# A spectral filter beside 32-head attention on one core: row transform by even and odd rows, Q's second half packed last, and new numbers in the planner

## The chip, the core and the metric

The kernel runs on one core of a Trainium2 chip. A core has five engines that run side by side, each with its own instruction queue: PE multiplies matrices and writes into PSUM (eight banks of 128 x 512 f32), ACT computes functions such as the exponential, DVE does elementwise work, POOL does slower elementwise work, and SP issues DMA transfers. The working memory is SBUF. The metric is the time of one launch on the device in microseconds; the kernel before takes 767.13 us, the median of three runs (766.32 to 768.4).

## The reference

Two independent computations stand beside each other in the output. A is a filter in the frequency domain; B is self-attention with 32 heads of width 20.

```python
def _A_ref(x, w_r, w_i):                       # x: (1, 2048, 640)
    X = rfft2(x.astype(float32), axes=(-2, -1))
    X = X * (w_r + 1j * w_i)                   # weights: (2048, 321)
    return irfft2(X, s=(S, D), axes=(-2, -1)).astype(bfloat16)

def _B_ref(x, wqkv, wo):                       # x: (1, 2048, 640)
    q, k, v = split_heads(x @ wqkv)            # 3 x 32 heads x (2048, 20)
    p = softmax(q @ k.T * 20 ** -0.5, axis=-1) # 2048 x 2048 per head
    return merge_heads(p @ v) @ wo

out = concatenate([a, b], axis=-1)
```

## The kernel before

The order of all instructions is written out ahead of time by a planner in the kernel's Python code. It plays the kernel through with a cost for each instruction, and at each moment puts on each engine what is ready and ranks first. What comes out is a fixed order for each engine, with semaphore waits where data cross engines. The costs decide only the order; the times in this document are the chip's.

**Attention.** There are 32 units, each of one quarter of Q's rows (512) and a group of four heads (list `UNITS`): first quarters 0 and 1 with groups 0 to 3, then quarter 0 and quarter 1 with groups 4 to 7, then quarters 2 and 3. A unit has 16 x 4 score tiles of 128 x 512. PE computes a tile with 32 of its 128 rows (`score_mm`, L821). Most tiles go in pairs to ACT for the exponential (`try_exp`, L1418). The rest go in batches of four to DVE, which builds the exponential from integer operations: four L955, one L998, one L997, one L1005. The product with V (L1076) uses 32 columns of PE per head. At the end of a unit DVE evicts the sum (L1107), the row sums go through DRAM and back as reciprocals (SP), POOL multiplies (L1128), and the output projection follows (L1222, L1233).

**Projection.** Heads 0 to 7 of K, and of the first two quarters of Q, are projected straight into place (L614). The rest is "packed": `packed` computes 128 columns of K or Q for 512 rows of x (five matmuls, L643), DVE evicts them into a staging buffer `stg` (L655), and when a column block is complete `spread_heads` sends each head's 20 rows to its place with a DMA. 34 packed jobs come in the order K1, Q1, K2, Q2, K3, Q3, K4, Q4 with four jobs each, and the last two row quarters of Q0; two staging buffers alternate. `kq_keys` says which pieces a score tile waits for. V is projected by L690. The transposes of x (L592) come ahead of all.

**Filter.** x is folded by POOL (L1630 to L1637), and when all packing is done and spread, the filter runs as background work: row transform S1 (L1736, evicted by L1742), column transform and weights S2 (L1793, L1824), inverse rows S3 (L1896; L1910, L1918, L1923), inverse columns S4 (L1948; L1956, L1967). S1 multiplies 1024 folded rows by four tables of cosine and sine for even and odd frequencies: 4 tables x 5 column blocks x 8 matmuls. Its jobs may start from due times that spread over `FT0` to `FT1` in proportion to the matmul cost. S3 already splits its table into two halves and gets the second half of its output as a difference, in mirrored order.

**Background work and the clock.** `step_pe` first feeds ACT, then uses the room until ACT needs the next pair for products with V, background jobs by priority, and tiles for DVE. Background jobs and DVE's tiles share four PSUM banks. If nothing else can be done and PE's work in the last `WIN` = 3413 ns is under `WARM` times `WIN`, `keep_warm` issues a matmul on constants (L1507), whose result nobody reads.

**SP's queue.** `step_aux` takes the first transfer whose data are there. `put_dma` counts 450 ns for each issue.

Of the kernel before, what the change touches and what calls it, by code (L numbers as in the profile page):

```python
# [255 lines left out]
S = 2048  # L256
D = 640
H = 32
# [39 lines left out]
class KB:  # L298
# [8 lines left out]
    WARM = 0.60  # L307
# [95 lines left out]
    def alloc_filter(self):  # L403
# [17 lines left out]
        self.VX = a.bf(zD + 8 * FBC, 4 * FBC).rearrange("p (s r l) -> p s r l", s=2, r=2)  # L421
        self.X24 = a.bf(zD + 16 * FBC, 8)
# [10 lines left out]
    def put(self, eng, fn, occ, r=(), w=(), pw=(), name="", lat=None, mode="B"):  # L433
        t = self.P.add(eng, fn, r=r, w=w, pw=pw, name=name)
        st = self.free[eng]
        if eng == "pe" and mode != self.mode:
            st += self.SW
            self.mode = mode
            self.switches += 1
        st = max(self.now, st)  # L440
        if eng == "pe":
            while (self.win + 1) * self.WIN + self.PHASE <= st:
                self.cold = self.wacc.get(self.win, 0.0) < self.COLD * self.WIN
                self.ncold += self.cold
                self.win += 1
            self.wacc[self.win] = self.wacc.get(self.win, 0.0) + occ
            self.plog.append((st, occ))
            if self.cold:
                occ *= 2.0
        if eng == "dve" and name in ("p2", "p3", "p4") and self.free["pool"] > st:  # L450
            occ += min(self.free["pool"] - st, 1.8 * occ) * 0.44
        end = st + occ
        self.free[eng] = end
        self.busy[eng] += occ
        if lat is None:
            lat = {"pe": self.L_PE, "act": self.L_ACT, "dve": self.L_DVE, "pool": self.L_POOL}[eng]
        t.vis = end + lat
        self.at(end)
        self.at(t.vis)
        return t  # L460

    def put_dma(self, fn, nbytes, r=(), w=(), pw=(), name="dma", stream=None, out=False):
# [7 lines left out]
        self.free["sp"] = st + 450.0  # L470
        self.dma_free = max(self.dma_free, st + 450.0) + nbytes / rate
        t.vis = self.dma_free + 1900.0
# [105 lines left out]
    def jobs_B(self):  # L578
# [56 lines left out]
        def packed(which, c, kc, sb, free):  # L635
# [15 lines left out]
            def mkev(bank):  # L651
                o = self.stg[sb][:, kc * 512:(kc + 1) * 512]
# [3 lines left out]
            ev = [(mkev, 610.0, [("z", "C", 0)], [("stg", which, c, kc)], [("stgb", sb, kc)], False)]  # L656
            return Job("pk%d" % which, 0.0, pe, ev)
        sb = 0
        hist = []
        order = [(1, 1), (0, 1), (1, 2), (0, 2), (1, 3), (0, 3), (1, 4), (0, 4), (0, 0)]  # L660
        for n_, (which, c) in enumerate(order):
                js = []
                free = hist[-2] if len(hist) >= 2 else []
                hist.append(self.spread_keys(which, c))
                for kc in (range(2, 4) if (which, c) == (0, 0) else range(4)):
                    j = packed(which, c, kc, sb, free)
                    j.prio = 1000.0 + 10 * n_ + kc
                    j.rel = self.PJ0 + self.PJ1 * (n_ + 0.25 * kc)
                    js.append(j)
                    J[("pk", which, c, kc)] = j  # L670

                def post(job, which=which, c=c, sb=sb, js=js):
                    if any(not x.done for x in js):
                        return
                    self.spread_heads(which, c, sb)
                for j in js:
                    j.post = post
                sb = (sb + 1) % 2
# [29 lines left out]
    def spread_keys(self, which, c):  # L708
        nm = ("QT", "KT")[which]
        ks = []  # L710
        for h in range(H):
            lo, hi = max(20 * h, 128 * c), min(20 * h + 20, 128 * c + 128)
            if lo < hi and not (which == 1 and h < 8):
                ks.append((nm + "h", h, c))
        return ks

    def spread_heads(self, which, c, sb):
        dst = (self.QT, self.KT)[which]
        nm = ("QT", "KT")[which]
        for h in range(H):  # L720
            lo, hi = max(20 * h, 128 * c), min(20 * h + 20, 128 * c + 128)
            if lo >= hi:
                continue
            g, j = divmod(h, 4)
            s0 = 0
            if g < 2:
                if which == 1:
                    continue
                s0 = 1024
            d0 = 32 * j + lo - 20 * h  # L730
            o = dst[d0:d0 + hi - lo, g, s0:2048]
            i_ = self.stg[sb][lo - 128 * c: hi - 128 * c, s0:2048]
            self.dma(o, i_, (hi - lo) * (2048 - s0) * 2, r=[(nm + "m", g)] + [("stg", which, c, kc) for kc in range(s0 // 512, 4)] + [("stgb", sb, kc) for kc in range(s0 // 512, 4)] + [("z", "C", 0)],
                     w=[(nm + "h", h, c)], name="spread")

    def kq_keys(self, u, kt):
        qc, g = UNITS[u]
        if g < 2:
            ks = [("KT", g, kt // 4)]
            if qc < 2:  # L740
                ks.append(("QT", g, qc))
            else:
                ks += [("QTh", h, c) for h in range(4 * g, 4 * g + 4) for c in range(20 * h // 128, (20 * h + 19) // 128 + 1)]
            return ks
        ks = []
        for h in range(4 * g, 4 * g + 4):
            c0, c1 = 20 * h // 128, (20 * h + 19) // 128
            for c in range(c0, c1 + 1):
                ks += [("KTh", h, c), ("QTh", h, c)]
        return ks  # L750
# [739 lines left out]
    def keep_warm(self):  # L1490
        t0 = self.now - self.WIN
        u = 0.0
        for st, occ in reversed(self.plog):
            if st + occ < t0:
                break
            u += min(occ, st + occ - t0)
# [50 lines left out]
    def step_aux(self, en):  # L1547
        lst = self.aux[en]
        for i, a in sorted(enumerate(lst), key=lambda x: x[1][6] != "onorm") if en == "pool" else enumerate(lst):
# [92 lines left out]
    def filter_tables(self):  # L1642
# [5 lines left out]
        for par in range(2):  # L1648
            k = 2 * np.arange(512, dtype=np.int64) + par
            ang = th * ((s[:, None] * k[None, :]) % S)  # L1650
            c_, n_ = np.cos(ang), np.sin(ang)
            m_ = -n_
            if par == 0:
                m_[:, 0] = alt
            for m in (c_, m_):
                t1.append(m.reshape(8, 128, 512).transpose(1, 0, 2))
# [42 lines left out]
    def jobs_A(self, after, need):  # L1699
# [16 lines left out]
        def load_x():  # L1716
            for i in range(2):
                self.dma(self.xf[i], self.xs[i].rearrange("(t p) d -> p t d", p=128), 1310720, r=[("xs", i, t) for t in range(8)], w=[("xf", i), zr("A", 0)], name="ld_xA")
# [6 lines left out]
        for idx in range(4):  # L1725
            ri, par = idx % 2, idx // 2
            b = idx % 2
            js = []
            for c in range(5):
                pe = []  # L1730
                for t in range(8):
                    def mk(bank, t=t, c=c, par=par, b=b):
                        o = ps[:, bank, :]
                        l = self.xf[par][:, t, c * 128:(c + 1) * 128]
                        r_ = self.tabs[b][:, t, :]
                        return lambda e: e.matmul(o, l, r_, start=(t == 0), stop=(t == 7))  # L1736
                    pe.append((mk, 216.0, [("xf", par), ("t1", idx), ("t1b", b), zr("A", 1), zr("C", 1)]))

                def mkev(bank, c=c, ri=ri, par=par):
                    o = self.X1[:, c, ri, par * 512:(par + 1) * 512]  # L1740
                    in_ = ps[:, bank, :]
                    return lambda e, en: e.tensor_copy(o, in_)  # L1742
                ev = [(mkev, 608.0, [zr("B", 1)], [("X1", c, ri, par), zr("B", 0)], [], False)]
                js.append(add(Job("S1", 0.0, pe, ev, after=after)))
            S1 += js
            if idx == 1:
                def fix():
                    x1 = self.X1
                    kk = [("X1", c, 1, 0) for c in range(5)]
                    self.pool_op(lambda e: e.tensor_copy(self.X24[:, 0:5], x1[:, :, 1, 0]), 120.0, r=kk + [zr("D", 2), zr("B", 1)], w=[("X24",), zr("D", 1)], name="x24")  # L1750
                    self.pool_op(lambda e: e.memset(x1[:, :, 1, 0], 0.0), 120.0, r=[("X24",), zr("B", 1)], w=kk + [("X1f",)], name="x24z")
                hook("fix", js, fix)
            if idx < 2:
                hook("ldt%d" % (idx + 2), js, (lambda idx: lambda: load_t(self.tabs, self.c_t1, idx + 2, 1, "t1", []))(idx))
# [29 lines left out]
        hook("ldfd", S1[10:15], load_fd)  # L1784
# [14 lines left out]
        for kc in range(9):  # L1799
            i = kc % 2  # L1800
            js = []
            M = 128 if kc < 8 else 1
            for pl in range(4 if kc < 8 else 2):
                sg, ri = divmod(pl, 2)
                if kc < 8:
                    if ri == 0:
                        terms = [(0, 0, t, t) for t in range(3)] + [(1 if sg == 0 else 2, 1, 2 + t, t) for t in range(3)]
                    else:
                        terms = [(0 if sg == 0 else 3, 1, t, t) for t in range(3)] + [(2, 0, 2 + t, t) for t in range(3)]
# [3 lines left out]
                for n, (tab, r_, c, t) in enumerate(terms):  # L1813
# [3 lines left out]
                    ks = [("X1", c, r_, kc // 4), ("X1f",)] if r_ < 2 else [("X24",), zr("D", 2)]  # L1817
# [8 lines left out]
                ev = [(mkev, 65 + 1.042 * 2 * FBC, wkeys(kc, sg) + [zr("D", 2)] + prevY_keys(kc), [(nm, sg), zr("D", 1)], [], False)]  # L1826
# [160 lines left out]
    FT1 = 745000.0  # L1987
# [141 lines left out]
    def build(self):  # L2129
# [7 lines left out]
        for h in range(H):  # L2137
            for c in range(20 * h // 128, (20 * h + 19) // 128 + 1):
                need.append(("QTh", h, c))
                if h >= 8:  # L2140
                    need.append(("KTh", h, c))
# [56 lines left out]
```

## Time and profile before

| | us |
|---|---|
| median of 3 runs | 767.13 |
| the profiled execution, whole | 769.53 |
| its span, first to last instruction | 767.7 |
| PE busy | 734.2 (96%) |
| ACT busy | 729.5 (95%) |
| DVE busy | 669.4 (87%) |
| POOL busy | 132.1 (17%) |

The groups of instructions that the change touches, from part 5 of the profile and the full table of groups:

| line, engine | what | count | busy us |
|---|---|---|---|
| L643 PE | packed projection | 170 weight loads | 44.8 |
| L1736 PE | row transform S1 | 160 weight loads | 41.8 |
| L1742 DVE | S1 evictions | 20 | 13.6 |
| L1507 PE | constant matmuls | 18 | 6.1 |
| L821 PE | scores | 2048 | 309.2 |

Some matmul records are missing from the trace (149 of L643, 140 of L1736), so the weight loads are counted. Durations of matmuls overlap, since each starts before the one ahead of it has drained; their sum says more than the time they take up. The stages of the filter stand one behind the other: S1 from 273 to 441 us, S2 to 528, S3 from 538 to 653, S4 from 660 on.

### The profile page before, as it was taken

The numbers are of one execution on the slowest core, as the hardware profiler recorded it, in microseconds if no ns is written. First come the engines' busy times: TensorE is split into PE (matmuls) and PEld (weight loads), VectorE is DVE, ScalarE is ACT, GpSimd is POOL, SyncE is SP. The second block draws the span as 40 slices with busy tenths as digits, with TensorE's granted clock in tenths as the row PEclk, the third lists the DMA queues.
The fourth block names the chain that finished last, engine by engine and source line by source line (L and its number), as shares of the span: only waits on it lengthen the run. The fifth ranks groups of instructions, "written<-read, shape, count | busy, mean of one in ns | idle before, by whom it ended". The sixth has DMA issues, their size and how long they took to land.

```text
span 767.7 us, 16364 instructions
## 1 busy us (share of the span) xinstructions
PE 734.2 (96%) x6532; PEld 237.0 (31%) x6591; DVE 669.4 (87%) x1234; ACT 729.5 (95%) x797; POOL 132.1 (17%) x142
## 2 busy tenths in 40 slices
PE   8999999999999999999999999999999999999997
PEld 4422233242332222232222333332232322333334
DVE  3598978989788989888989999999998889899895
ACT  5899989999899999999999999999999999999992
POOL 7388840000000000003100121210000000000000
PEclk9999989999999999999999999999999999999999
DMA  9022322110212351212120111212001110211102
GB/s 317 14 68 84 91 74 63 35 47 21 62 33 44 93 216 29 71 45 100 35 72 22 43 51 29 55 35 99 24 20 46 38 31 18 74 56 37 54 19 72
DMA packets 43009, 46.76 MB, mean 61 GB/s; under 512 B 16470, under 2 KB 36312, under 8 KB 42416
## 3 DMA queue, kind: packets, MB, share of 16 engines
q1 hardware_dynamic: 42160, 44.35, 19.1%
q0 software_dynamic: 768, 1.32, 0.7%
q8 instruction: 53, 0.87, 0.5%
q14 instruction: 28, 0.23, 0.1%
HBM read 30.57 MB, written 8.36 MB: 51 GB/s over the span
## 4 chain that ended last, share of the span: by engine, by line
ACT 65%; PE 26%; DVE 6%; DMA 1%; issue 1%; SPq 0%
ACT arena L1418 65%; PE ps L821 8%; PE ps L1076 6%; DVE arena L955 2%; PE ps L1793 2%; PE ps L614 2%; PE ps L690 2%; PE ps L643 2%; PE ps L1222 1%; DVE arena L998 1%; PE ps L1896 1%; DMA arena<-ct 1%; DVE arena L997 1%; PE ps L1948 1%; PE ps L572 1%
## 5 line engine op out<-in xcount | busy, mean ns | idle before, releaser
L1418 ACT ACTIVATE arena<-ps 128x1024 f16<-128x1024 f32 x784 | 722.3, 1126 | 15.8 <-PE ps L821 12.3
L955 DVE TENSOR_SCALAR arena<-ps 128x512 int16<-128x512 f32 x480 | 320.5, 683 | 45.2 <-PE ps L821 43.0
L821 PE MATMUL ps<-arena 32*128 32x512 bf16 x2048 | 309.2, 385 | 13.4 <-ACT arena L1418 8.8
L1076 PE MATMUL ps<-arena 128*32 128x512 f16 x3008 | 236.0, 386 | 1.7 <-DVE arena L998 0.3
L821 PEld LDWEIGHTS ps<-arena 32*128 32x128 bf16 x2048 | 76.2, 91 | 297.4 <-ACT arena L1418 274.9
L1128 POOL TENSOR_TENSOR arena<-arena 128x512 bf16<-128x512 f32 x30 | 39.3, 1309 | 499.3 <-DMA arena<-rd 499.2
L998 DVE TENSOR_SCALAR arena<-arena 128x2048 int16<-128x2048 int16 x120 | 91.0, 758 | 1.4
L997 DVE TENSOR_SCALAR arena<-arena 128x2048 int16<-128x2048 int16 x120 | 86.7, 723 | 3.5 <-PE ps L1076 2.8
L1076 PEld LDWEIGHTS ps<-arena 128*32 128x32 bf16 x3008 | 50.5, 94 | 96.4 <-issue 65.9
L643 PE MATMUL ps<-arena 128*128 128x512 bf16 x149 | 44.8, 383 | 2.2 <-issue 1.7
L1736 PE MATMUL ps<-arena 128*128 128x512 bf16 x140 | 41.8, 383 | 3.4 <-issue 2.4
L1793 PE MATMUL ps<-arena 128*128 128x322 bf16 (+1 forms) x198 | 37.7, 303 | 0.2 <-DVE arena L955 0.2
L1948 PE MATMUL ps<-arena 128*128 128x320 bf16 (+1 forms) x192 | 34.6, 302 | 0.0
L690 PE MATMUL ps<-arena 128*128 128x160 bf16 x320 | 31.3, 240 | 1.6 <-DVE arena L955 1.5
L1896 PE MATMUL ps<-arena 128*128 128x512 bf16 (+3 forms) x121 | 29.8, 332 | 2.1 <-issue 1.3
L1824 DVE TENSOR_TENSOR arena<-ps,arena 128x644 bf16<-128x644 f32 (+1 forms) x34 | 27.9, 822 | 2.1 <-PE ps L1793 1.7
L1005 DVE TENSOR_SCALAR arena<-arena 128x96 bf16<-128x96 bf16 x120 | 29.3, 245 | 0.0
L1222 PE MATMUL ps<-arena 128*128 128x320 bf16 (+1 forms) x152 | 28.2, 302 | 0.6 <-DVE arena L955 0.4
L690 PEld LDWEIGHTS ps<-arena 128*128 128x128 bf16 x320 | 22.3, 100 | 13.2 <-issue 10.4
L696 DVE CAST arena<-ps 128x320 bf16<-128x320 f32 x32 | 15.5, 488 | 11.9 <-PE ps L690 11.8
L655 DVE TENSOR_SCALAR arena<-ps 128x512 bf16<-128x512 f32 x34 | 23.1, 679 | 2.7 <-PE ps L643 2.5
L1107 DVE COPY arena<-ps 128x512 f32<-128x512 f32 (+1 forms) x33 | 21.9, 666 | 1.5 <-PE ps L1076 1.4
(77 smaller groups left out, 354.0 us busy)
## 6 DMA issues: line engine op xcount, KB each, us to landing
arena<-rd SPq DMA_DIRECT2D x120, 64.0 KB
out_dram<-arena SPq DMA_DIRECT2D x32, 160.0 KB
arena<-ct SPq DMA_DIRECT2D x4, 1024.0 KB
arena<-arena SPq DMA_DIRECT2D x42, 80.0 KB
arena<-in_A_x_dram SPq DMA_DIRECT2D x16, 160.0 KB
xs<-arena SPq DMA_DIRECT2D x16, 160.0 KB
arena<-xs SPq DMA_DIRECT2D x2, 1280.0 KB
arena<-arena SPq DMA_DIRECT2D x105, 20.0 KB
```

Source lines behind the costliest of these rows:

```text
L643: return lambda e: e.matmul(o, l, r_, start=(cc == 0), stop=(cc == 4))
L690: return lambda e: e.matmul(o, l, r_, start=st, stop=(c == 4), skip_group_check=True)
L821: return e.matmul(self.ps[:, bank, :], self.KT[32 * j:32 * j + 32, g, kt * 128:(kt + 1) * 128], self.QT[32 * j:32 * j + 32, g, qc * 512:(q ...
L955: return e.tensor_scalar(o, in_, 0.0, 31744.0, ALU.max, ALU.min)
L997: self.dve_push([(lambda e, en: e.tensor_scalar(Ii, Ii, SH2, 0.0, ALU.subtract, ALU.max), occ, ik + pk, ik, [], "p3")], lambda: push(self. ...
L998: ops = [(lambda e, en: e.tensor_scalar(Gi, Ii, SH1, 0.0, ALU.subtract, ALU.max), occ, ik, [("G", b)], [], "p2")]
L1076: inst = e.matmul(self.ps[32 * j:32 * j + 32, bank, :], v_, p_, start=s_, stop=False, tile_position=(0, 32 * j), skip_group_check=True)
L1128: self.pool_op(lambda e: e.tensor_tensor(on, of, bc, ALU.mult), 1600.0, r=pk + [("bcu", u, j) for j in range(4)] + [("bc", j) for j in ran ...
L1418: self.put("act", lambda e: e.activation(o, in_, AF.Exp, bias=ACT_BIAS, scale=ACT_SCALE), 0.8333 * 512 * n + 60.0, r=[("ps", b) for b in b ...
L1736: return lambda e: e.matmul(o, l, r_, start=(t == 0), stop=(t == 7))
L1793: return lambda e: e.matmul(o, lhs, r_, start=st, stop=sp)
L1948: return lambda e: e.matmul(o, l, r_, start=(n == 0), stop=(n == 5))
```

## The change

The change has four parts.

1. **S1** is split by the parity of the row. A frequency k and its mirror 1024 - k have the same sum over even rows and the opposite sum over odd rows (signs aside). So each table now holds 256 cosines and 256 sines for even rows and the same for odd rows: two tables of 1 MB in place of four. For each parity of k and each of five column blocks there are two jobs of four matmuls. The even job is copied to an f32 buffer `sb1`; the odd job's PSUM bank is added to it (first half of the output) and subtracted from it (second half, in mirrored order). For even k three operations on one column go with it. `X24`, which POOL copied before, is written by one of these. In S2 two signs change for the mirrored half.
2. **Packing**: the order becomes K1, the first half of Q1, K2, first half of Q2, and so on to 4, and then the second halves of Q0 to Q4. K has one staging buffer, Q's halves use parts of both. A head of Q is spread by two transfers, one for each half, where it was one.
3. **Planner's DMA costs**: issue times by kind (`ISSUE`), later arrival for some kinds (`LATE`), and an order of kinds in SP's queue (`FIRST`).
4. **Constant matmuls**: a score group counts half (`fillA` 0.5) in the work of the last window, and `WARM` goes from 0.60 to 0.55. `FT1` goes from 745 to 700 us.

```diff
-    WARM = 0.60
+    WARM = 0.55
...
+        self.sb1 = a.f32(zD, 512)
...
-            self.plog.append((st, occ))
+            self.plog.append((st, occ, 0.5 if name == "fillA" else 1.0))
...
+    ISSUE = {"spread": 770.0, "packO": 770.0, "sum": 290.0, "bcast": 465.0}
+    LATE = {"sum2": 1500.0, "spread": 800.0, "ld_tab": 1000.0, "ld_W": 1000.0, "bcast": 500.0}
+    FIRST = {"sum": 0, "sum2": 0, "rec2": 0, "bcast": 0, "spread": 2}
...
-        self.free["sp"] = st + 450.0
-        self.dma_free = max(self.dma_free, st + 450.0) + nbytes / rate
-        t.vis = self.dma_free + 1900.0
+        oc = self.ISSUE.get(name, 530.0)
+        self.free["sp"] = st + oc
+        self.dma_free = max(self.dma_free, st + oc) + nbytes / rate
+        t.vis = self.dma_free + 1900.0 + self.LATE.get(name, 0.0)
...
-        order = [(1, 1), (0, 1), (1, 2), (0, 2), (1, 3), (0, 3), (1, 4), (0, 4), (0, 0)]
-        for n_, (which, c) in enumerate(order):
+        last = {}
+        order = []
+        for c in range(1, 5):
+            order += [(1, c, (0, 1, 2, 3), 0, 0), (0, c, (0, 1), 1, 2 * (c % 2))]
+        order += [(0, c, (2, 3)) + sl for c, sl in enumerate(((1, 2), (0, 0), (0, 2), (1, 0), (1, 2)))]
+        for n_, (which, c, kcs, sb, s0) in enumerate(order):
                 js = []
-                free = hist[-2] if len(hist) >= 2 else []
-                hist.append(self.spread_keys(which, c))
-                for kc in (range(2, 4) if (which, c) == (0, 0) else range(4)):
-                    j = packed(which, c, kc, sb, free)
+                sl = {kc: s0 + i for i, kc in enumerate(kcs)}
+                free = sorted({k for i in sl.values() for k in last.get((sb, i), ())})
+                last.update({(sb, i): self.spread_keys(which, c, kcs) for i in sl.values()})
+                for kc in kcs:
+                    j = packed(which, c, kc, sb, sl[kc], free)
                     j.prio = 1000.0 + 10 * n_ + kc
-                    j.rel = self.PJ0 + self.PJ1 * (n_ + 0.25 * kc)
+                    j.rel = self.PJ0 + self.PJ1 * 0.25 * sum(k[0] == "pk" for k in J)
...
-        for st, occ in reversed(self.plog):
+        for st, occ, wt in reversed(self.plog):
             if st + occ < t0:
                 break
-            u += min(occ, st + occ - t0)
+            u += wt * min(occ, st + occ - t0)
...
+            k = 2 * np.arange(256, dtype=np.int64) + par
+            m = []
+            for e in range(2):
+                se = s[e::2]
+                ang = th * ((se[:, None] * k[None, :]) % S)
+                c_, m_ = np.cos(ang), -np.sin(ang)
+                if par == 0:
+                    mid = th * ((se * 512) % S)
+                    m_[:, 0] = np.rint(np.cos(mid)) if e == 0 else np.rint(np.sin(mid))
+                m.append(np.concatenate([c_, m_], 1))
+            t1.append(np.concatenate(m, 0).reshape(8, 128, 512).transpose(1, 0, 2))
...
+                for e in range(2):
+                    pe = []
+                    for n in range(4):
...
+                            return lambda e: e.matmul(o, l, r_, start=(n == 0), stop=(n == 3))
+                        pe.append((mk, 216.0, [("xf", par, e)] + t1k))
+                    if e == 0:
+                        def mkev(bank):
+                            return lambda e, en: e.tensor_copy(sb1, ps[:, bank, :])
+                        ev = [(mkev, 608.0, prev + [zr("D", 2)], [("sb1", c, par), ("sb1",)], [] if prev else [zr("D", 1)], False)]
+                    else:
...
+                        def e1(bank, X=X, o0=o0):
+                            return lambda e, en: e.tensor_tensor(X[:, :, o0:o0 + 256], ps[:, bank, :].rearrange("p (r k) -> p r k", r=2), sv, ALU.add)
...
+                            return lambda e, en: e.tensor_tensor(X[:, :, 1023:767:-1], sv, i_, ALU.subtract)
...
+                        ev.append((e2, 608.0, kr, [("X1r", c, par)], zw, False))
+                        prev = [("X1r", c, par)]
...
-    FT1 = 745000.0
+    FT1 = 700000.0
```

## Prediction, before the changed kernel was run

> **What bounds the kernel now.** I read the page first. One line of its part 2 and two of part 5:
>
> ```profile
> ACT  5899989999899999999999999999999999999992
> ...
> L1418 ACT ACTIVATE arena<-ps 128x1024 f16<-128x1024 f32 x784 | 722.3, 1126 | 15.8 <-PE ps L821 12.3
> L955 DVE TENSOR_SCALAR arena<-ps 128x512 int16<-128x512 f32 x480 | 320.5, 683 | 45.2 <-PE ps L821 43.0
> ```
>
> ACT computes exponentials almost without a break: 784 of them fill 722.3 us, so one costs 722.3/784 = 0.921 us and covers two score tiles. It is idle 15.8 us before them. The other 480 of the 2048 tiles are done by DVE in batches of four. A batch costs DVE four L955 (4 x 0.67 us), one L997 and one L998 (0.72 + 0.76) and one L1005 (0.24), 4.4 us in all, and spares ACT two exponentials, 1.84 us. PE shows 96% busy, but matmul records overlap; what tells is that ACT waited for it only 12.3 us.
>
> So three things make the span: the number of exponentials, the gaps between them, and the ends before the first and after the last. ACT's own timeline shows the gaps, as pieces with the wait before each in brackets:
>
> ```profile
> 96.45 1.94 ACT L1418 ACTIVATE arena<-ps 128x1024 f16<-128x1024 f32 x2 [0.49 <-PE ps L821]
> 99.95 1.02 ACT L1418 ACTIVATE arena<-ps 128x1024 f16<-128x1024 f32 x1 [1.56 <-PE ps L821]
> ...
> 211.69 62.44 ACT L1418 ACTIVATE arena<-ps 128x1024 f16<-128x1024 f32 x68 [3.92 <-PE ps L821]
> 274.33 232.58 ACT L1418 ACTIVATE arena<-ps 128x1024 f16<-128x1024 f32 x253 [0.21 <-PE ps L821]
> 508.68 68.18 ACT L1418 ACTIVATE arena<-ps 128x1024 f16<-128x1024 f32 x74 [1.77 <-PE ps L1076]
> 577.07 173.92 ACT L1418 ACTIVATE arena<-ps 128x1024 f16<-128x1024 f32 x189 [0.22 <-PE ps L1076]
> ```
>
> Exponentials run from 13.40 to 751.0 us. The gaps that matter are six between 96 and 106 us (0.49 + 1.56 + 0.49 + 0.16 + 0.50 + 0.57 = 3.8 us), one at 208 us (3.9) and one at 507 us (1.8); 3.8 us more lie before 37 us, in the start-up. After 751.0 come 16.7 us. The timeline of the end:
>
> ```profile
> 758.64 4.25 PE L1948 MATMUL ps<-arena 128*128 128x320 bf16 x30
> 758.83 0.43 ACT L1233 CAST arena<-ps 128x320 bf16<-128x320 f32 x1 [1.22 <-PE ps L1227]
> ...
> 762.93 1.01 DVE L1967 TENSOR_TENSOR arena<-arena,ps 128x320 bf16<-128x320 f32 x2
> ```
>
> Attention's last eviction (L1233) ends at 759.26. What ends last is the filter: 30 matmuls of its last stage are left over until attention is through, the last eviction ends at 763.94, and the store behind it closes the span at 767.7.
>
> **Row transform by even and odd rows.** Today 160 matmuls of 512 columns (L1736). In the timeline three such in a row take 0.82 us and two 0.60, so one more costs 0.22. 80 go away: 80 x 0.22 = 17.6 us of PE. None of it is on ACT's path by itself; it lies between 273 and 441 us, where ACT waits for nothing. What it buys is room: the filter's work is fed into PE's gaps, by due times from 200 to 745 us, and it runs late. Before and after are the planner's intended starts, from the job costs in the code (34.6 us, 27.1, 23.0, 26.1 by stage): the last stage is due from 200 + 545 x 84.7/110.8 = 617 us and starts at 660. With 17.3 us in the first stage and an end at 700 it is due from 200 + 500 x 67.4/93.5 = 560. The first stage took 168 us for 160 matmuls; at the same pace 80 take 84. The other stages keep their lengths (90, 123 and 105 us), so the filter ends some 80 us earlier, or at its due time near 700: in both cases before attention does. The leftover after 758.64 then goes. Late next is attention's own store: 759.26 plus the 3.76 us that the last store now takes from its eviction to the end gives 763.0. **Minus 4.7 us.** From below: 0, if the filter stays late; from above nothing more, as the attention tail remains.
>
> The price is on DVE. Twenty copies (L1742, 13.6 us) become ten copies, ten sums and ten mirrored differences, and 15 operations of one column. The third stage of the filter is already built so, and its rows price them: copy L1910 0.680, sum L1918 0.681, difference L1923 0.680, one column L1913 0.150 us. 30 x 0.68 + 15 x 0.15 = 22.6, plus 9.0 us. The 4.5 us of evictions now done after 759 us also move in beside attention. From 273 to 751 us DVE is busy 150.0 + 85.2 + 111.7 + 87.4 = 434.4 of 478 us, 90.9%. To keep all 480 tiles it would have to do 434.4 + 13.5 = 448 us, 93.7%. If the share stays at 90.9%, 13.5/4.4 = 3.1 batches go back to ACT: plus 5.6 us. If it rises to the 94.7% of the fullest stretch (85.24 of 90 us, 442 to 532), there is room for one batch more: minus 1.8. DVE's largest wait is for L821 score matmuls, 43.0 us in 74 waits, and a lighter PE shortens just these; so I take the middle, one batch lost. **Plus 1.8 us.** The two table loads that go away (2 MB) and one POOL copy (0.58 us) cost nothing now: ACT's gap at 274 us is 0.21.
>
> **Q's second half last.** The gap at 208 us is a wait for data. Attention's unit 8 (first quarter of Q, heads 16 to 19) needs the packed projection of columns 256 to 511 of K and Q. In today's order that is job 24 of 34. Weight loads of L643 by windows (five to a job) put its end at 206 us, and its spread transfers and the arrival behind it: ACT resumes at 211.69. Job 18, where the new order has the same data for the first half of Q, was through at 183 us. That is 23 us of margin against a stall of 3.9, so it goes. **Minus 3.9 us.** Nothing else is moved ahead of it: the V jobs keep their places by priority. The second half is first read by unit 16; at 22.6 us a unit (49 tiles x 0.46) that is near 13 + 16 x 22.6 = 375 us, while all packing is over at 254 today. The K staging buffer becomes single: K of the next column block can't be evicted before the last one's seven transfers have landed, about 7 x 0.77 + 3 = 8 us. Two Q jobs and V jobs stand between, and today a job takes (206 - 63)/24 = 6 us, so I cost it at nothing; without that cover it is 8 us for each of three blocks, spread over a margin of 23.
>
> Every transfer is issued by SP. Splitting Q makes 36 + 27 = 63 spread transfers into 27 + 27 + 36 = 90. The queue's rows show twelve of them in 9.17 us, 0.76 each: 27 x 0.76 = 20.6 us more of SP between 62 and 265 us. SP is free there about a third of the time (in a stretch of 22 us a unit costs it some 7.5 us, the 63 spreads add 5 us, loads and stores of the folded input 2). What could be queued behind is the chain of row sums and reciprocals. The new order of SP's queue puts these first and spreads last, so it is cost at nothing. Only POOL's L1128 waits for that chain (499.2 us in 28 waits, nobody behind it in a hurry).
>
> **Issue times and constant matmuls.** The measured issue costs and lateness change only the order that is planned. Where the planner counts a transfer later than it counted it before, it moves other work ahead instead of stalling; no row prices this. It could save the small unplanned gaps (0.2 + 0.2 us) or add as much: nothing.
>
> The rule for constant matmuls bears on the gaps at 96 to 106 us. The windows (PEclk behind the engines' busy times):
>
> ```profile
> 96.00:98.00 2.00, 1.28 (x17) 0.32 (x13) 2.00 (x3) 1.54 (x2) 2.00 (x2) 1.00 0.01 4
> 98.00:100.00 2.00, 1.61 (x12) 0.91 (x16) 2.00 (x4) 0.44 (x2) 1.85 (x3) 0.60 0.00 0
> 100.00:102.00 2.00, 2.00 (x16) 0.51 (x9) 0.13 (x1) 1.51 (x2) 1.92 (x4) 0.50 0.36 115
> ```
>
> The granted clock falls to half for some 6 us, and ACT loses 3.8 us. The Trainium skill, "TensorE: Matmul & The Clock Gate", section "Why this matters for your kernels", says that the clock is kept by having no idle gap of more than about 3 us between bursts of matmuls. By that rule no constant matmul is needed here, and the change would win nothing: the longest wait of PE ahead of the drop is 1.1 us. The row speaks otherwise: the clock fell although PE was 64% busy in the 2 us before. The measurement decides, so a stricter count is worth something. Score matmuls (L821) will count half. There are 3413/921 = 3.7 of these groups in a window, so the count falls by 0.5 x 0.22 x 3.7 = 0.41 us or 12% of the window, while the threshold falls by 5%: stricter by 7%, about one matmul more per window where the count is marginal. 18 are there now (L1507). I expect dozens, in gaps only, at no price to ACT. The section's first rule speaks against the change as a whole, since it thins PE's work by 17.6 us; a second drop of the clock would cost another 3.8. Ends: minus 3.8 and plus 3.8 us. I take half the gain, since the same place is now guarded. **Minus 1.9 us.**
>
> **Sum.** -4.7 + 1.8 - 3.9 - 1.9 = -8.7 us. The profiled execution took 769.53 us, 767.7 of span and 1.8 around it; its span becomes 759.0. The median shown is 767.13, 2.4 under that execution; the same difference gives 758.4.
>
> **Rivals.** (1) PE's relief becomes DVE tiles: with DVE at 94.7% plus the now empty 50 us at the end, four batches more instead of one less, 5 x 1.84 = 9.2 us lower, 749. For it: the 43.0 us of waiting. Against it: only one stretch is that full now. (2) Nothing that lasts: the filter still ends last and another load takes the gap at 208, so 8.6 us of the gains fall away and 767 stays. For it: the filter has run behind its due times throughout. Against it: 84 us of slack in my own sum. (3) DVE becomes the bound. Between 273 and some 360 us the odd half's PSUM bank is held through up to five operations (0.68 x 2 + 0.15 x 3 = 1.8 us against 0.68), the next even half waits for the one f32 buffer, and DVE's own tiles find no bank. Without the tile term the gains are 10.5 us, so it decides from the sixth lost batch (6 x 1.84 = 11.0). With eight lost: 767.1 - 10.5 + 14.7 = 771.3. For it: DVE is at 89 to 95% already. Against it: the filter's third stage has the same form and got 85 tiles in 123 us, 0.69 per us, close to the 0.76 of the first stage now; at that rate 84 us lose 6 tiles, not 32.
>
> **Chances.** The forecast 0.55 (751 to 764 us), rival 1 0.18, rival 2 0.09, rival 3 0.18. A measurement of this kernel tells 0.3% (2.3 us) from no change. Faster 0.55 + 0.18 = 0.73, same 0.09, slower 0.18. The range starts at 744, where rival 1 has one and a half batches more than its number, and ends at 768, leaving out rival 3 and little else; the forecast's own range is 751 to 764.
>
> **What would show it.** Right: no gap of ACT over 1 us near 208 us; L1948 over before the last exponential, and a tail under 13 us; 80 row-transform matmuls over by about 350 us; L955 between 465 and 490; a granted clock of 1.00 from 60 to 750 us. Wrong: fewer than 456 tiles by DVE (rival 3), over 490 (rival 1), or filter stores still last (rival 2).

## The result, and the profile after

The changed kernel takes 758.0 us (median of four runs, 757.3 to 760.62) where the kernel before takes 767.31 (four runs, 766.32 to 768.4): the ratio is 0.9885, with a 95% interval of 0.9858 to 0.9912. Five more runs of it in the experiments, beside 23 of the kernel before, gave 0.9899 (0.9875 to 0.9922). Forecast were 758.4 us. The profiled execution took 758.05 us, its span is 756.2, 11.5 less than before. One run of all those in this document (776.22 us, with the old issue times) lay more than 1.5% above the fastest of its kernel, and its ratio leaves it out.

From the page after, the line of ACT in 40 slices and the two groups that share the score tiles (busy us and mean ns, then idle before and its releaser):

```profile
ACT  5899999999999999999999999999999999999994
...
L1413 ACT ACTIVATE arena<-ps 128x1024 f16<-128x1024 f32 x784 | 722.6, 1115 | 9.4 <-PE ps L816 7.4
L950 DVE TENSOR_SCALAR arena<-ps 128x512 int16<-128x512 f32 x480 | 320.3, 682 | 30.5 <-PE ps L816 26.9
```

The split of the tiles is exactly as before, 784 exponentials and 480 tiles on DVE. ACT works no less, it only waits less. Its own timeline after, at the places where it waited before:

```profile
97.08 3.81 ACT L1413 ACTIVATE arena<-ps 128x1024 f16<-128x1024 f32 x4 [0.56 <-PE ps L816]
101.21 145.87 ACT L1413 ACTIVATE arena<-ps 128x1024 f16<-128x1024 f32 x158 [0.32 <-PE ps L816]
247.34 85.36 ACT L1413 ACTIVATE arena<-ps 128x1024 f16<-128x1024 f32 x93 [0.26 <-PE ps L816]
...
384.32 1.02 ACT L1413 ACTIVATE arena<-ps 128x1024 f16<-128x1024 f32 x1 [0.51 <-PE ps L816]
...
497.84 246.58 ACT L1413 ACTIVATE arena<-ps 128x1024 f16<-128x1024 f32 x268 [0.57 <-PE ps L816]
```

From 101 to 247 us it runs on with no gap over 0.12 us, straight across the place of the 3.9 us gap. The last piece ends at 744.42. The timeline of the end, after:

```profile
751.14 0.71 PE L1217 MATMUL ps<-arena 128*128 128x320 bf16 x4
751.83 0.30 PE L1222 MATMUL ps<-arena 80*128 80x320 bf16 x1
752.16 0.43 ACT L1228 CAST arena<-ps 128x320 bf16<-128x320 f32 x1 [1.22 <-PE ps L1222]
752.61 0.33 SPq L486 DMA_DIRECT2D out_dram<-arena  x1
```

There is no matmul of the filter's last stage (L1977 now) among them; that stage's last weights were loaded at 710.3 us. Attention's own store ends the run.

ACT's timeline, added up for every kernel of this study, shows where each one's span comes from. The columns are the start of the first exponential, the sum of all gaps between exponentials (also of those too short to show in the timeline), the end of the last one, the tail behind it and the span, in us; all are of profiled executions. Experiments are named by what they leave out of the changed kernel or add to the one before.

| kernel | exponentials | start | gaps | last ends | tail | span |
|---|---|---|---|---|---|---|
| before | 784 | 13.4 | 15.3 | 751.0 | 16.7 | 767.7 |
| after | 784 | 12.9 | 8.9 | 744.4 | 11.8 | 756.2 |
| after, second time | 784 | 13.8 | 9.0 | 745.3 | 11.7 | 757.0 |
| after, old row transform | 780 | 13.1 | 10.4 | 742.3 | 26.4 | 768.7 |
| after, old packing | 784 | 12.8 | 14.0 | 748.6 | 12.2 | 760.8 |
| after, old DMA costs | 784 | 13.0 | 16.0 | 752.3 | 12.1 | 764.4 |
| after, no order of kinds on SP | 784 | 13.8 | 9.3 | 745.0 | 11.2 | 756.2 |
| after, no lateness | 784 | 13.8 | 5.6 | 740.7 | 11.3 | 752.0 |
| after, old issue times | 782 | 13.0 | 17.7 | 752.2 | 11.3 | 763.5 |
| after, old DMA costs, late sums | 788 | 13.5 | 13.8 | 752.6 | 11.5 | 764.1 |
| after, old constant matmuls | 784 | 13.7 | 10.3 | 746.5 | 12.1 | 758.6 |
| after, due times to 745 | 782 | 13.6 | 11.5 | 746.2 | 15.1 | 761.2 |
| before, new row transform | 786 | 13.1 | 10.6 | 746.6 | 13.5 | 760.2 |
| before, new packing | 786 | 13.4 | 14.0 | 752.5 | 20.8 | 773.3 |

Before to after: 4.9 us of the tail, 6.4 of the gaps and 0.5 of the start, less 0.3 of busy time (722.6 for 722.3), make the 11.5.

### The profile page after: what moved, and what is told of

It is laid out like the page before. It is cut to its first block, busy times and chain, and to the rows that moved or that the text cites. A ratio compares the mean times of both kernels' runs of the same rounds, so it can differ in the third digit from the quotient of the medians.

```text
span 756.2 us, 16333 instructions
## 1 busy us (share of the span) xinstructions
PE 722.5 (96%) x6488; PEld 231.9 (31%) x6537; DVE 676.2 (89%) x1259; ACT 729.8 (97%) x797; POOL 132.1 (17%) x141
## 4 chain that ended last, share of the span: by engine, by line
ACT 62%; PE 27%; DVE 9%; issue 1%; DVEq 0%
ACT arena L1413 62%; PE ps L816 9%; PE ps L1071 7%; DVE arena L950 3%; PE ps L1821 2%; PE ps L649 2%; PE ps L1217 2%; PE ps L698 2%; DVE arena L993 1%; PE ps L620 1%; DVE arena L992 1%; DVE arena L1000 1%; DVE arena L1853 1%; PE ps L1977 1%; PE ps L578 1%
## 5 line engine op out<-in xcount | busy, mean ns | idle before, releaser
L1413 ACT ACTIVATE arena<-ps 128x1024 f16<-128x1024 f32 x784 | 722.6, 1115 | 9.4 <-PE ps L816 7.4
L950 DVE TENSOR_SCALAR arena<-ps 128x512 int16<-128x512 f32 x480 | 320.3, 682 | 30.5 <-PE ps L816 26.9
L816 PE MATMUL ps<-arena 32*128 32x512 bf16 x2048 | 308.6, 384 | 13.6 <-ACT arena L1413 8.1
L649 PE MATMUL ps<-arena 128*128 128x512 bf16 x148 | 44.4, 383 | 2.7 <-issue 1.9
L1977 PE MATMUL ps<-arena 128*128 128x320 bf16 (+1 forms) x192 | 35.7, 302 | 0.0
L1000 DVE TENSOR_SCALAR arena<-arena 128x96 bf16<-128x96 bf16 x120 | 32.5, 270 | 0.0
L1217 PE MATMUL ps<-arena 128*128 128x320 bf16 (+1 forms) x152 | 28.8, 302 | 0.6 <-DVE arena L950 0.6
L698 PEld LDWEIGHTS ps<-arena 128*128 128x128 bf16 x320 | 21.3, 98 | 14.6 <-issue 9.8
L1738 PE MATMUL ps<-arena 128*128 128x512 bf16 x70 | 21.4, 383 | 1.6 <-issue 1.3
L704 DVE CAST arena<-ps 128x320 bf16<-128x320 f32 x32 | 15.5, 486 | 7.3 <-PE ps L698 7.2
```

The lines of the kernel that those rows point to most:

```text
L649: return lambda e: e.matmul(o, l, r_, start=(cc == 0), stop=(cc == 4))
L698: return lambda e: e.matmul(o, l, r_, start=st, stop=(c == 4), skip_group_check=True)
L816: return e.matmul(self.ps[:, bank, :], self.KT[32 * j:32 * j + 32, g, kt * 128:(kt + 1) * 128], self.QT[32 * j:32 * j + 32, g, qc * 512:(q ...
L950: return e.tensor_scalar(o, in_, 0.0, 31744.0, ALU.max, ALU.min)
L1000: self.dve_push([(lambda e, en: e.tensor_scalar(vs, vi, W1, None, ALU.mult), 105.0, [("V", g // 2, kt), ("Vone",), ("Vpad",)], vk, [], "vs ...
L1217: return lambda e: e.matmul(o, ot[0:M, c, qb * 128:(qb + 1) * 128], self.wo[0:M, c, half * 320:(half + 1) * 320], start=(c == 0), stop=(c ...
```

## The experiments

Every kernel was compared with the kernel before on the same chip; its medians there were 765.75, 766.17 and 765.78 us. The edits are cut to the lines that say what differs; comments in them are added.

**The row transform taken back.**

```diff
-    for par in range(2):      # 2 tables x 5 blocks x 2 row parities x 4 matmuls
+    for idx in range(4):      # 4 tables x 5 blocks x 8 matmuls
```

> The changed kernel with the row transform of before (160 matmuls, four tables); packing, DMA costs, constant matmuls and the end of the due times stay as changed. The order that this plans has 488 tiles on DVE and 1560 on ACT (780 exponentials) where the changed kernel has 480 and 784. Theory (what the split transform bought is the tail): the filter ends last again, +4.7 us at the end, and 4 exponentials less, -3.7 us: 759. Rival (PE's relief is what closed the gaps between exponentials): the gaps come back as well, 3 to 6 us, and the time is 762 to 765.

Measured: 772.67 us (770.54 to 780.26), ratio 1.0105 (1.0073 to 1.0137), slower than the kernel before. Both numbers were too low. The four exponentials less are there (the last ends at 742.3, the earliest up to then), the gaps grow by 1.5 us only, but the tail is 26.4 us. The timeline of its end:

```profile
750.74 1.01 DVE L1961 TENSOR_TENSOR arena<-arena,ps 128x320 bf16<-128x320 f32 x2 [1.15 <-PE ps L1942]
750.81 12.98 PE L1942 MATMUL ps<-arena 128*128 128x320 bf16 x94
...
763.02 2.05 DVE L1961 TENSOR_TENSOR arena<-arena,ps 128x320 bf16<-128x320 f32 x4 [0.17 <-PE ps L1942]
```

94 matmuls of the filter are left when attention is through, where the kernel before left 30. Nothing else in the table makes 14.6 us (26.4 - 11.8). Why more than before? The same 160 matmuls of the row transform, in the kernel before and here (shortest, median and longest weight load in ns, then the start of the first and the last in us):

```profile
L1736 PEld LDWEIGHTS ps<-arena x160: 95/98/99, 273.1 to 439.4; 128*128 128x128 bf16 x160
...
L1730 PEld LDWEIGHTS ps<-arena x160: 95/98/99, 293.6 to 459.4; 128*128 128x128 bf16 x160
```

They take as long, but begin 20 us later. The filter starts when all packing is done and spread, and the new packing order ends later (last weights at 267.7 us, 252.6 before). The first filter matmul comes at 270 to 279 us in the three kernels with the old order, at 284 to 304 us in all with the new one. So the filter is a second bound beside ACT, the new order pushes it back, and without the split it takes back all that the other parts win.

**The packing order taken back.**

```diff
-        for c in range(1, 5):
-            order += [(1, c, (0, 1, 2, 3), 0, 0), (0, c, (0, 1), 1, 2 * (c % 2))]
+        order = [(1, 1), (0, 1), (1, 2), (0, 2), (1, 3), (0, 3), (1, 4), (0, 4), (0, 0)]
```

> The changed kernel with the packing order of before (Q whole, 24 jobs ahead of unit 8). Theory: ACT's gap near 208 us comes back with 3 to 5 us and the time is 762. Rival (the better DMA issue times alone let the planner arrange the transfers so that unit 8 has its data): no gap over 1 us there and 758.

Measured: 764.22 us (762.6 to 766.01), ratio 0.9974 (0.996 to 0.9988). The theory's gap came back, and larger, but not where I put it. The timeline around it:

```profile
248.49 3.83 PE L1513 MATMUL ps<-arena 128*128 128x512 bf16 x17
...
252.54 0.61 PE L827 MATMUL ps<-arena 32*128 32x512 bf16 x7 [0.22 <-DMA arena<-arena]
252.97 1.94 ACT L1424 ACTIVATE arena<-ps 128x1024 f16<-128x1024 f32 x2 [7.14 <-PE ps L827]
```

ACT stands for 7.1 us while PE does the last packed projections and then 17 constant matmuls (L1513): the planner has no score tile with data there and fills the time. The tile that ends it waits last for a transfer between SBUF places, a spread. At 208 us there is no gap over 0.15. So the order is worth some 5 us in this plan (764.2 against 758.9), and the wait has no fixed place: with the old DMA costs too it ended at 211.7 us in the kernel before and at 204.5 with the row transform alone.

**The constant matmuls as before.**

```diff
-    WARM = 0.55
+    WARM = 0.60
-            self.plog.append((st, occ, 0.5 if name == "fillA" else 1.0))
+            self.plog.append((st, occ))
```

> The changed kernel with the constant matmuls of before (every matmul counts fully, threshold 0.60); 32 constant matmuls where the changed kernel has 44. Theory: the granted clock falls to half again near 96 to 106 us or in another thin place, ACT loses 3.8 us, 762. Rival (the clock fell because of the order of work in that place, which the new packing has changed anyway): clock 1.00 throughout and 758.

Measured: 760.99 us in ten runs (757.97 to 764.27), ratio 0.9934 (0.9913 to 0.9955). The runs are of two kinds: five with a mean granted clock of 0.990 to 0.993 took 763.0 us in the mean, five with 0.997 to 0.999 took 759.1. The difference is 3.8 us, as much as ACT's gaps at 96 to 106 us in the kernel before. Its profiled execution is of the second kind, so no line of it shows the drop, and where in the run the clock falls stays open.

**The changed kernel once more.** No edit.

> The changed kernel once more, on this chip, beside the others, to count in how many executions the clock falls. The ratio of its first runs (0.9885) times 765.75 us gives 757. Theory (the changed count of constant matmuls keeps the clock up): the granted clock is 0.996 or more in at least four of five executions, while without that count four of ten were. Rival (the count does nothing): it falls in about half of them, and the median is 759 to 761.

Measured: 758.85 us (758.1 to 759.6), clock 0.998 to 1.0 in all five; with the first four runs it is one drop (0.992, 760.62 us) in nine executions, against five in ten (the "four of ten" that kept the clock in the text above were five). The theory holds in direction; the numbers are small for a share. The median is 2 us higher than 757, within what the two intervals allow.

**Due times of the filter up to 745 us.**

```diff
-    FT1 = 700000.0
+    FT1 = 745000.0
```

> The changed kernel with due times of the filter up to 745 us as before; 484 tiles on DVE. Theory: the filter's last stage reaches past the last exponential, so its last store ends the run, up to 4.7 us later, less 1.8 us for two exponentials: 758 to 761. Rival (the halved row transform alone takes the filter off the end): tail as in the changed kernel, and 756.

Measured: 759.42 us (758.66 to 763.04), ratio 0.9914 (0.9898 to 0.993), inside the theory's span and not clear of the changed kernel (758.85). The mechanism is there: the filter's last weights are loaded at 756.1 us and its tail is 15.1. The opposite edit, 700 us in the kernel before, plans instruction for instruction the same order on every engine; it is no change there. The filter is behind its due times in that kernel, so they bind nothing. The profiled execution is slower (763.04 us) for another reason. Windows, with PEclk after the engines' busy times:

```profile
500.00:502.00 2.00, 2.00 (x13) 0.29 (x9) 1.43 (x4) 1.03 (x2) 0.00 (x0) 0.50 0.30 107
502.00:504.00 2.00, 2.00 (x9) 0.33 (x6) 1.04 (x2) 1.41 (x2) 0.00 (x0) 0.50 0.55 157
```

The clock is at half around 500 us, and ACT (fourth pair) computes 1.0 to 1.4 us of each 2.

**The row transform alone, in the kernel before.** The edit is the first one, the other way round.

> The kernel before with the split row transform alone; the order planned has 476 tiles on DVE (786 exponentials). Theory (before, the filter's end and ACT's end were two bounds side by side, and the split takes the filter's away): the tail after the last exponential shrinks from 16.7 to about 12 us, the gap near 208 us stays, 2 exponentials more cost 1.8: 763 to 764. Rival (PE's relief alone also fills ACT's gaps): 758 to 760.

Measured: 762.33 us (760.87 to 766.39), ratio 0.9947 (0.993 to 0.9965). The theory's parts are there: ACT's gap is 3.92 us as before (it ends at 204.5 us), two exponentials more, a tail of 13.5. This profiled execution lacks the drop of the clock near 100 us (its own lies at 473 to 480 us), and that is most of its 4.7 us less of gaps. The rival falls.

**The packing order alone, in the kernel before.** The edit is the second one, the other way round.

> The kernel before with the new packing order alone; 476 tiles on DVE (786 exponentials). Theory (the filter ends last whatever ACT gains): ACT has no gap over 1 us near 208 and its last exponential ends earlier by 2 us, but the filter's last store ends where it did: 765 to 768, no gain. Rival (the gains add up as in the prediction's sum): 765.75 - 3.9 + 1.8 = 763.7.

Measured: 775.4 us (775.18 to 777.6), ratio 1.0125 (1.01 to 1.0151). Neither had it: this part alone costs 9 us. The gap near 208 us is gone, but another of 5.9 us stands at 265, and the tail is 20.8 us. From the timeline of its end:

```profile
758.98 9.17 PE L1937 MATMUL ps<-arena 128*128 128x320 bf16 x66
```

66 filter matmuls are left, since the filter starts at 288.6 us here, 15.5 later than before. The gap is that of the next experiment.

**The DMA costs and SP's order taken back.**

```diff
-    ISSUE = {"spread": 770.0, "packO": 770.0, "sum": 290.0, "bcast": 465.0}
-    LATE = {"sum2": 1500.0, "spread": 800.0, "ld_tab": 1000.0, "ld_W": 1000.0, "bcast": 500.0}
-    FIRST = {"sum": 0, "sum2": 0, "rec2": 0, "bcast": 0, "spread": 2}
+        self.free["sp"] = st + 450.0
```

> The changed kernel with the DMA costs and SP's order of before (450 ns for each issue, no lateness, first ready first). Theory (they only change a plan that had slack): 757, ACT idle before its exponentials 9 to 10 us as in the changed kernel. Rival (with wrong issue times the planner hands PE score tiles whose data have not landed): unplanned waits of 2 to 4 us more on ACT, named as waits for PE on a transfer, 759 to 761.

Measured: 767.64 us (765.24 to 773.07), ratio 1.0026 (1.0005 to 1.0046). My theory falls: this part is worth 8.8 us of the changed kernel. The rival has the kind of fault, but at less than half the price, and it is DVE that waits for the transfer. The timeline from 248 us on shows how:

```profile
247.89 12.44 SPq L481 DMA_DIRECT2D arena<-arena  x15
252.67 0.68 DVE L1097 COPY arena<-ps 128x512 f32<-128x512 f32 x1
...
260.44 1.24 SPq L481 DMA_DIRECT2D sd<-arena  x4
261.72 3.65 SPq L481 DMA_DIRECT2D arena<-arena  x5
265.54 0.35 SPq L481 DMA_DIRECT2D arena<-sd  x1
...
267.10 0.25 DVE L1112 RECIPROCAL arena<-arena 128x16 f32<-128x16 f32 x1 [5.65 <-DMA arena<-sd]
268.55 1.04 PE L1066 MATMUL ps<-arena 128*32 128x512 f16 x8 [5.28 <-DVE arena L987]
270.17 2.10 ACT L1408 ACTIVATE arena<-ps 128x1024 f16<-128x1024 f32 x2 [5.67 <-PE ps L811]
```

DVE has evicted the row sums of a unit (L1097) at 253.4, but SP writes them to DRAM only at 260.4: fifteen transfers between SBUF places stand ahead in its order and take 12.44 us, 0.83 each. The planner counted 450 ns for each, so these alone are 15 x 0.38 = 5.7 us late, as long as the wait that follows. Five spreads more (3.65 us) stand between the write and the reading back at 265.5; part of that time the sums need anyway to land (in the changed kernel 2.35 us pass between such a write, at 249.0, and its reading, at 251.4). The planner had put the reciprocal into DVE's order where it thought the sums had landed, and DVE, which takes its instructions in order, stands on it for 5.65 us. PE waits for DVE, ACT for PE. Then the clock falls:

```profile
264.00:266.00 2.00, 0.00 (x0) 0.00 (x0) 0.00 (x0) 0.49 (x1) 0.00 (x0) 1.00 0.18 42
266.00:268.00 2.00, 0.00 (x0) 0.00 (x0) 0.90 (x3) 0.00 (x0) 0.00 (x0) 0.83 0.21 45
268.00:270.00 2.00, 1.45 (x11) 0.25 (x11) 1.19 (x3) 0.00 (x0) 0.00 (x0) 0.50 0.10 16
```

All 12 runs of this kernel have a clock of 0.985 to 0.995. In the kernels with the old packing (before, and the row transform alone) the reciprocal never waits for its sums. It does so with the new packing and old costs, 9.2 us in three waits here and 8.4 in three with the packing alone. The 27 transfers more lengthen SP's queue; whether their number or their new order makes the wait was not separated.

Which of the three numbers matters? Three kernels leave out one each, and a fourth, whose edit is against the kernel with the old DMA costs, puts a single number in their place.

```diff
-    FIRST = {"sum": 0, "sum2": 0, "rec2": 0, "bcast": 0, "spread": 2}
+    FIRST = {}
```

> The changed kernel without the order of kinds in SP's queue (issue times and lateness stay); 480 tiles on DVE. If the order is what keeps the row sums from queuing behind the spread transfers, the stall of DVE on the reciprocal near 265 us is back with 4 to 6 us and the clock falls after it: 765 to 768. If the planned costs alone do it, no wait of the reciprocal over 1 us: 758 to 760.

Measured: 756.1 us (754.89 to 758.0), ratio 0.986 (0.9842 to 0.9878), not slower than the changed kernel. SP's order is not what does it; no wait of the reciprocal is listed.

```diff
-    LATE = {"sum2": 1500.0, "spread": 800.0, "ld_tab": 1000.0, "ld_W": 1000.0, "bcast": 500.0}
+    LATE = {}
```

> The changed kernel without the lateness by kind (issue times and SP's order stay); 480 tiles on DVE. If the lateness is what puts the reciprocal behind the landing of its sums in DVE's order, the reciprocal waits for the transfer in many units, 0.5 to 1.5 us each where SP is not crowded, and DVE loses tiles' time: 762 to 768. If not: 758 to 760.

Measured: 753.97 us (753.54 to 756.13), ratio 0.9845 (0.9823 to 0.9868), the fastest kernel here and below both that were compared: without the lateness the plan is better. It has the same 784 exponentials, a tail of 11.3 us and gaps of 5.6 us, all but 2.3 of these before 38 us. That the lateness is harmful as such isn't shown; it's one plan against another.

```diff
-        oc = self.ISSUE.get(name, 530.0)
+        oc = self.ISSUE.get(name, 450.0)   # and ISSUE = {}
```

> The changed kernel with 450 ns for each issue (lateness and SP's order stay); 484 tiles on DVE (782 exponentials, 1.8 us less of ACT). If the issue times are what matters while 90 spread transfers are issued, the stall is back and the time is 763 to 768. If they are not, 756 to 758, and it is the fastest kernel here.

Measured: 765.19 us in ten runs (762.61 to 776.22), ratio 0.999 (0.9964 to 1.0017), although it has two exponentials less. The reciprocal's wait is back, 9.0 us in three waits, the longest 6.0 at 283 us: the sums evicted at 268.8 us are written at 276.4, behind twelve transfers of 8.9 us. The clock stays at half from 282 to 299 us. Of the three numbers, the issue times are the one without which the loss is back; that they do it alone, with neither of the other two, was not run.

```diff
-    LATE = {}                 # old issue times, old order of SP
+    LATE = {"sum2": 6000.0}
```

> The changed kernel with the old DMA costs and the old order of SP, and one number in their place: the read-back of the row sums counts 6 us later, so that the reciprocal stands that much later in DVE's order. If the 8.8 us between the two come from DVE standing still on that reciprocal, the 5.7 us gap of ACT near 265 us and the fall of the clock after it go, and the time is 758 to 762. If they come from elsewhere (the spread transfers themselves), it stays at 765 to 768.

Measured: 765.57 us in ten runs (762.89 to 768.73), ratio 1.0004 (0.9982 to 1.0027). No wait of the reciprocal is left, so the edit did what it says, and still the time stays. Its plan has 788 exponentials, 4 x 0.92 = 3.7 us more, and ACT has a gap of 4.0 us up to 285.6, where PE stands before the filter's first matmul:

```profile
284.01 1.01 PE L1738 MATMUL ps<-arena 128*128 128x512 bf16 x2 [3.64 <-issue]
...
285.60 1.02 ACT L1413 ACTIVATE arena<-ps 128x1024 f16<-128x1024 f32 x1 [4.02 <-PE ps L816]
```

The profile names no releaser for PE there. That it is the load of x or of a table, which the planner again counted too short, fits (the DMA engines' share is 0.97 in the two microseconds before) but isn't shown. So the experiment leaves open how much of the 8.8 us the reciprocal alone is worth; a wrong issue time shows up wherever an in-order engine meets a transfer.

## Why the prediction was right, and where its working was wrong

The total was right: -8.7 us forecast, -9.3 in the first runs and -7.3 in the later ones (766.17 to 758.85). Of the mechanism, the tail and the gap at 208 us came as forecast. The other two terms, +1.8 for DVE and -1.9 for the clock, are each nearly nothing when medians are compared; that they cancel is luck.

- **The tail, -4.7 us.** Measured 16.7 to 11.8, -4.9. The mechanism was right: the filter leaves the end. The 80 matmuls took from 297 to 379 us, 81 us, for 84 forecast. They began 24 us later than before, so "over by about 350" was wrong by that: the new order packs until 267 us, not 253, and the filter waits for it. The prediction put this at nothing. It took the slack of the filter for granted; the two kernels with the new order and the old row transform, with tails of 26.4 and 20.8 us, show its price.
- **DVE, +1.8 us.** The split's price was right, 6.8 + 6.8 + 6.8 us in the large operations and 0.7 x 3 in the small ones, 22.5 for 22.6 forecast. The old row transform in the changed kernel has eight tiles more on DVE, two batches for the 9 us. But the count did not fall against the kernel before: DVE's waits for score matmuls fell from 43.0 to 26.9 us. The term is 0.
- **The gap at 208 us, -3.9.** Gone, as forecast. That nothing else pays for it was wrong, see below.
- **The clock, -1.9.** In the profiled executions the gaps at 96 to 106 us went from 3.8 to 0.9 us (0.56 + 0.32), and the clock stays up. But I took half of a drop that I had read from one execution, and most runs of the kernel before have none: in the 63 runs beside the experiments the clock is below 0.997 in six. That profiled execution was 2.4 us over its median for this reason (four of the 63, at 0.995, are 2.8 us over the median of their 23). Against the median of before the term is nearly nothing; in the changed order of work the stricter count may be worth the 2 us between 761.0 and 758.9, but the intervals of the two ratios overlap.
- **Gaps that I left alone.** The one at 507 us (1.8 us) is gone too; new ones of 0.5 to 0.6 us stand at 384 to 386 and at 497.
- **Slips without weight.** DVE's evictions after 759 us are 4.0 us, not 4.5. The range's lower end of 744 lies 5 us under rival 1, which is nearly three batches and not one and a half.

The step that failed, though the total hides it, is "The measured issue costs and lateness change only the order that is planned", costed at nothing, with its companion that only POOL waits for the chain of row sums. DVE's reciprocal stands in that chain, and DVE takes its work in order. The term was worth 8.8 us, as a condition: with the old DMA costs the changed kernel is no faster than the one before (767.64 us, ratio 1.0026). The wait of DVE, 9.2 us in three places, is shown; how much of the 8.8 it makes by itself is open, as the last experiment says.

The other fault is the form of the sum. I added gaps and tail as if independent. ACT's end and the filter's end are two bounds side by side. With the old row transform everything else together ends 1% later than before (772.7 us); the packing order alone ends 9 us later; the row transform alone wins 0.5% of the 1.0 to 1.15%. The whole gain comes only from the parts together, which a sum of single terms can't show.

## What to carry to other kernels

Where two streams share the engines, find the end of each before adding savings: what one gains counts only up to where the other ends, and work moved to the back of one stream can hold up the start of the other. Where the order of instructions is planned ahead, a cost that is too low in the plan isn't harmless, as each engine stands still on the first instruction whose data are late; measure the issue time of a transfer when the number of transfers grows. Before a stall of one profiled execution is charged, look at whether the runs around it have it.

## What the runs showed of the hardware

A granted clock of half came while PE stood still for 5.3 us (263.3 to 268.5 us in the kernel with old DMA costs; the 0.83 of the window from 266 us puts the fall near 267.3), and also with PE never idle for more than 1.1 us (at 98 us in the kernel before). The drop does not come in every execution of the same kernel: the mean clock is below 0.997 in six of 63 runs of the kernel before, and at 0.993 or less in five of ten with the old count of constant matmuls, where the place of the drop is not shown. These five were 3.8 us longer than the other five. The profiled drops last from 7 us (98 to 105 us, before) to 17 us (282 to 299 us, old issue times).

A transfer between SBUF places kept SP for 0.73 to 0.83 us, the write of a row of sums to DRAM for 0.31 (1.24 us for four).
